# The product with w_out by groups of four token tiles, four of its seven products split once more, in matmuls of 192 columns

## The chip, the cores and the metric

One core of a Trainium2 chip. The metric is the device time of one execution in microseconds (us), and all numbers are from executions on the chip. Every run told here was in its fast state. An engine is called PE (TensorE, the matmuls), PEld (TensorE loading weights), DVE (VectorE), ACT (ScalarE), POOL (GpSimd) or SP (the queue that issues transfers).

## The reference, cut to what matters

Attention over 8 batches, 12 heads and 448 positions gives x with 3584 tokens of 768 numbers; the second half of the kernel is a feed-forward block:

```python
def _moe_ref(x, w_in, w_out):          # (3584, 768), (768, 2048), (2048, 768)
    h = x @ w_in
    g = h * (1.0 / (1.0 + np.exp(-h)))
    return (g @ w_out).astype(np.float32)
```

This case is about the last line, `g @ w_out`, in float32.

## The kernel before

A product of two matrices, each cut in 2 x 2 blocks, needs eight products of blocks. There is a form with seven products and some additions (Strassen's, in Winograd's order), and the kernel uses it for both x @ w_in and g @ w_out. `left_sums` and `right_sums` form the sums of blocks on VectorE; `Seven` runs the seven products, adds them up as they leave PSUM, and takes its PSUM banks from `bank`, which at this point of the kernel rotates over six of them:

```python
    order = ["mm", "mm", "sc", "sc", "av0", "av1"]
    def bank(n):                                    # ... (the case used earlier is cut)
        name = order[0]
        order.append(order.pop(0))
        ...
    class Seven:
        def product(self, name):
            t, ends = bank(self.n), (self.steps[0], self.steps[-1])
            for s in self.steps:
                nc.tensor.matmul(t, self.left(name, s), self.right(name, s), start=s == ends[0], stop=s == ends[1])
                yield self.n
            return t
        def five(self):
            ...
            plus((yield from self.product("6")), p1, u2)
            nc.scalar.copy(p5, (yield from self.product("5")))
            plus((yield from self.product("7")), u2, u3)
            nc.gpsimd.tensor_tensor(out=u2, in0=u2, in1=p5, op=ALU.add)
            nc.gpsimd.tensor_tensor(out=done[2, 2], in0=u3, in1=p5, op=ALU.add)
            plus((yield from self.product("3")), u2, done[1, 2])
            plus((yield from self.product("4")), u3, done[2, 1])
```

For w_out a pair of token tiles (256 tokens) is taken at a time. A block of the left side is 128 tokens by 1024 hidden numbers, so a product is eight matmuls of 128 rows and 384 columns:

```python
    def halves_out(t):
        w = tiles[t % 2].rearrange("p (m r t c) -> p m r t c", m=HF, r=2, t=2)
        ...
        left_sums(a11, a12, a21, a22, s[:, 0], s[:, 1], s[:, 2])
        ...
        steps = [2 * i + k for i in ORDER for k in range(2)]
        part = Seven(lambda name, m: lefts[name][:, m], right, steps, z.HALF, done)
        yield from chain(part.two(), part.five())
        # ... stores
    for t in range(NT // 2):                        # 14 pairs
        for _ in halves_out(t):
            pass
        fetch(t + 2)
```

Of the kernel before, what the change touches and what calls it, by code (L numbers as in the profile page):

```python
# [11 lines left out]
F32 = mybir.dt.float32  # L12
AF = mybir.ActivationFunctionType
ALU = mybir.AluOpType
# [13 lines left out]
BANK = 512  # L28
# [413 lines left out]
def store(nc, out, z, column, o, m0, *queues):  # L442


    at, queues = 0, queues or [nc.sync]
    while at < o.shape[0]:
        b, c = divmod(column + at, z.S)
        j, p = divmod(c, z.R)
        n = min(z.R - p, o.shape[0] - at)
        rows = out[ds(b * z.S, z.S), ds(m0, o.shape[1])].rearrange("(p j) m -> j p m", j=z.J)  # L450
        queues[0].dma_start(rows[j, ds(p, n)], o[ds(at, n), :])
        queues = queues[1:] + queues[:1]
        at += n
# [3 lines left out]
def bounded(  # L457
# [3 lines left out]
    P, D, R, J, S = z.P, z.D, z.R, z.J, z.S  # L461
    HW, HF = z.NW // 2, z.NF // 2
    mem = ctx.enter_context(tc.tile_pool(name="mem", bufs=1))
    ps = ctx.enter_context(tc.tile_pool(name="ps", bufs=1, space=bass.MemoryType.PSUM))
    dram = ctx.enter_context(tc.tile_pool(name="dram", bufs=1, space=bass.MemoryType.DRAM))
    NC, loads, place, norm, spare, ones, first = (
        own[name] for name in ("NC", "loads", "place", "norm", "spare", "ones", "first")
    )
# [4 lines left out]
    hidden = dram.tile([z.NF, P, z.B * S], F32, name="hidden")  # L473


    sets = [mem.tile([P, 2 * z.NW * S], F32, name=f"x{i}") for i in range(2)]
    sums_x = mem.tile([P, 3 * HW * S], F32, name="sums_x")
# [3 lines left out]
    at = 0  # L481
# [42 lines left out]
    def weights(c, j):  # L524

        return other if j == 0 and c < GROUP and c % 2 else e[j]
# [41 lines left out]
    def scores(c, j, i=None):  # L568


        banks = ps.tile([P, 2, BANK], F32, name="sc", bufs=2)
        for half in range(2):
            pair = half if j == LEFT else i
            keys = kT[:, ds((z.KA, z.KB)[0 if j == LEFT else i] + j * P, P)]
            for h in range(2):
                rows = ds(h * D, D)
                nc.tensor.matmul(  # L577
                    banks[ds(half * D, D), h, 0:S], keys[rows, ts(half, D)], qT[rows, pair, :],
                    start=True, stop=True,
                )  # L580
        for h in range(2):
            nc.scalar.activation(  # L582
                eleft[:, h] if j == LEFT else weights(c, j)[:, i, h], banks[:, h, 0:S], AF.Exp,
                scale=norm.column(c, i, h, j),
            )

# [111 lines left out]
    def minus(a, b, out):  # L698
        nc.vector.tensor_tensor(out=out, in0=a, in1=b, op=ALU.subtract)

    def plus(a, b, out):
        nc.vector.tensor_tensor(out=out, in0=a, in1=b, op=ALU.add)  # L702

    def left_sums(a11, a12, a21, a22, s1, s2, s4, steps=range(4)):

        for step in steps:
            (
                lambda: plus(a21, a22, s1),
                lambda: minus(s1, a11, s2),
                lambda: minus(a11, a21, a21),  # L710
                lambda: minus(a12, s2, s4),
            )[step]()
# [22 lines left out]
    class Seven:  # L735
# [9 lines left out]
# [3 lines that stand above are left out]
                nc.tensor.matmul(  # L748
                    t, self.left(name, s), self.right(name, s), start=s == ends[0], stop=s == ends[1]
                )  # L750
                yield self.n
            return t
# [158 lines left out]
    def chunk_out(i):  # L911

        w = home[i][0].rearrange("p (m r h k) -> p m r h k", m=2, r=2, h=2)
        s = home[i][1].rearrange("p (s m k) -> p s m k", s=3, m=2)
        return (
            w[:, :, 0, 0], w[:, :, 0, 1], w[:, :, 1, 0], w[:, :, 1, 1], s[:, 0], s[:, 1], s[:, 2]
        )

    def prepare_out(m):

        if m == HF // 2:
            fetch(0)
        for _ in range(room.CHUNK):
            rounder.open()
            yield
            rounder.round()
        if m % 2:
            right_sums(*chunk_out(ORDER[m // 2]))
        yield

    NT = z.B * S // P
    size = z.NF * 2 * P
    tiles = [work[:, ds(0, size)], sets[1][:, ds(0, size)]]
    s_tiles = [work[:, ds(size, 3 * HF * P)], sums_x[:, ds(0, 3 * HF * P)]]
    outs = [stage[:, ds(i * z.DM, z.DM)] for i in range(3)]
    outs += [room.chunk(3)[:, ts(i, z.DM)] for i in range(3)]

    def fetch(t):

        if t >= NT // 2:  # L940
            return
        dst = tiles[t % 2].rearrange("p (f c) -> p f c", f=z.NF)
        nc.sync.dma_start(
            dst, hidden[:, :, ds(t * 2 * P, 2 * P)].rearrange("f p c -> p f c")
        )

    def halves_out(t):
        w = tiles[t % 2].rearrange("p (m r t c) -> p m r t c", m=HF, r=2, t=2)
        s = s_tiles[t % 2].rearrange("p (s m c) -> p s m c", s=3, m=HF)
        a11, a12, a21, a22 = (w[:, :, i, j] for j in range(2) for i in range(2))  # L950
        left_sums(a11, a12, a21, a22, s[:, 0], s[:, 1], s[:, 2])
        lefts = {"1": a11, "2": a12, "3": s[:, 2], "4": a22, "5": s[:, 0], "6": s[:, 1], "7": a21}

        def right(name, m):
            b11, b12, b21, b22, t1, t2, t4 = chunk_out(m // 2)
            return {"1": b11, "2": b21, "3": b22, "4": t4, "5": t1, "6": t2, "7": b12}[name][
                :, m % 2
            ]

        o = [outs[(2 * t + i) % len(outs)] for i in range(2)]  # L960
        done = {(i + 1, j + 1): o[i][:, ts(j, z.HALF)] for i in range(2) for j in range(2)}
        steps = [2 * i + k for i in ORDER for k in range(2)]
        part = Seven(lambda name, m: lefts[name][:, m], right, steps, z.HALF, done)
        yield from chain(part.two(), part.five())
        for i in range(2):
            if t < NT // 2 - 1 or i == 0:
                store(nc, out, z, (2 * t + i) * P, o[i], 0)
            else:
                for j in (1, 0):
                    store(  # L970
                        nc, out, z, (2 * t + i) * P, o[i][:, ts(j, z.HALF)], j * z.HALF,
                        nc.scalar, nc.sync,
                    )


    filler = dict(work=iter(()), due=0.0, share=0.0)
# [179 lines left out]
        begun[m] = rows, part_in(group, m, rows)  # L1156
        run(begun[m][1].two())
    run(halves_in(group, range(HF), prepare_out, begun))
    fetch(1)
    for t in range(NT // 2):  # L1160
        for _ in halves_out(t):
            pass
        fetch(t + 2)


@with_exitstack
# [207 lines left out]
```

## Time and profile before

| | |
|---|---|
| median of the first three runs | 1422.76 us (1421.24 to 1424.42) |
| span of the profiled run | 1424.3 us |
| stage of w_out, first to last product | 913.5 to 1419.2 us: 505.7 us |
| PE in that stage | busy without a gap |
| DVE in that stage (913 to 1419 us) | 105.7 us busy of 506 |

The stage is read from the chain of waits: a product on PE starts where the last one ended. PE therefore sets the time, and DVE has room. The lines are in the prediction below.

### The profile page before, as it was taken

How to read it: one execution, taken by the hardware profiler on the slowest of the kernel's cores; microseconds unless marked ns; L12 is line 12 of the kernel's file. 1: busy time of each engine (PE TensorE's matmuls, PEld its weight loads, DVE VectorE, ACT ScalarE, POOL GpSimd, SP SyncE). 2: the span in 40 equal slices, each digit the busy share in tenths (PEclk: the TensorE clock that was granted, in tenths of full speed). 3: DMA queues.
4: the chain of work that ended last, by engine and by line, in shares of the span. 5: the costliest groups of instructions: out<-in, count | busy, mean ns of one | idle time of the engine just before them, and what ended most of it. 6: DMA issues, size and time to landing. Idle time of an engine off the chain costs nothing.

```text
span 1424.3 us, 16665 instructions
## 1 busy us (share of the span) xinstructions
PE 1385.2 (97%) x6273; PEld 704.1 (49%) x6273; DVE 659.7 (46%) x917; ACT 492.5 (35%) x802; POOL 365.5 (26%) x261
## 2 busy tenths in 40 slices
PE   7998999999999999999999999999999999999998
PEld 4333444444444444444444455555555555555554
DVE  3886876765645445645444776622212222222220
ACT  5875555645455445455444344200000000000000
POOL 4764442433223223223221344300000000000000
PEclk9999999999999999999999999999999999999999
DMA  7654434332223223223211465422222222222210
GB/s 179 187 152 111 120 104 144 83 94 77 76 79 95 75 84 91 77 80 93 65 53 58 152 221 177 147 91 81 81 80 82 79 77 77 73 81 74 79 53 26
DMA packets 170814, 139.22 MB, mean 98 GB/s; under 512 B 102884, under 2 KB 151396, under 8 KB 170724
## 3 DMA queue, kind: packets, MB, share of 16 engines
q1 hardware_dynamic: 170656, 138.01, 33.0%
q8 instruction: 52, 0.85, 0.3%
q14 instruction: 38, 0.31, 0.1%
q10 hardware_dynamic: 68, 0.05, 0.0%
HBM read 88.47 MB, written 41.29 MB: 91 GB/s over the span
## 4 chain that ended last, share of the span: by engine, by line
PE 88%; DVE 6%; ACT 2%; issue 2%; SPq 1%; DMA 1%; POOL 0%; DVEq 0%; ACTq 0%
PE mm L748 38%; PE sc L748 15%; PE av L748 14%; PE av L609 9%; PE sc L577 8%; DVE work L652 2%; PE sc L544 1%; PE sc L559 1%; PE sc L643 1%; PE mm L643 1%; DVE work L623 1%; ACT work L582 1%; DVE rms L396 1%; DVE W L116 1%; DVE stage L702 0%
## 5 line engine op out<-in xcount | busy, mean ns | idle before, releaser
L748 PE MATMUL mm<-x,W 128*128 128x448 f32 x654 | 264.3, 549 | 10.7 <-DVE stage L702 7.5
L582 ACT ACTIVATE work<-sc,rms 128x448 f32<-128x448 f32 x324 | 184.1, 632 | 86.4 <-PE sc L577 78.2
L424 POOL TENSOR_TENSOR rms<-rms,minus_half 128x14 f32<-128x14 f32 (+4 forms) x55 | 138.6, 2522 | 254.5 <-DVE rms L420 201.1
L748 PE MATMUL mm<-sums_x,W 128*128 128x448 f32 x474 | 190.5, 542 | 2.3 <-DVE stage L702 1.5
L748 PEld LDWEIGHTS mm<-x,W 128*128 128x128 f32 x654 | 122.2, 192 | 138.8 <-issue 109.0
L577 PE MATMUL sc<-work 64*64 64x448 f32 x1344 | 165.6, 550 | 6.9 <-ACT work L582 5.0
L609 PE MATMUL av<-work,rows 64*64 64x448 f32 x1296 | 153.8, 549 | 7.9 <-issue 2.8
L623 DVE TENSOR_TENSOR work<-work 128x896 f32<-128x896 f32 (+1 forms) x114 | 123.3, 1114 | 76.4 <-ACT work L582 75.6
L748 PEld LDWEIGHTS mm<-sums_x,W 128*128 128x128 f32 x474 | 88.6, 190 | 91.7 <-issue 83.2
L763 POOL TENSOR_TENSOR parts<-parts,stage 128x448 f32<-128x448 f32 (+1 forms) x36 | 47.7, 1324 | 328.4 <-DVE parts L702 328.4
L609 PEld LDWEIGHTS av<-work,rows 64*64 64x64 f32 x1296 | 52.2, 134 | 97.4 <-issue 87.9
L577 PEld LDWEIGHTS sc<-work 64*64 64x64 f32 x1344 | 51.9, 134 | 89.4 <-issue 38.7
L763 POOL TENSOR_TENSOR parts<-parts,W 128x384 f32<-128x384 f32 x9 | 8.9, 993 | 307.5 <-DVE parts L702 307.5
L396 DVE TENSOR_REDUCE rms<-squares 112x8 f32<-112x512 f32 (+1 forms) x80 | 52.4, 655 | 68.1 <-ACT squares L395 67.3
L748 PE MATMUL sc<-W,work 128*128 128x384 f32 x204 | 68.6, 486 | 0.0
L881 ACT ACTIVATE stage<-stage 128x896 f32<-128x896 f32 x63 | 57.2, 945 | 25.9 <-DVE stage L702 25.3
L755 ACT COPY stage<-mm 128x448 f32<-128x448 f32 (+1 forms) x29 | 15.3, 528 | 143.5 <-PE mm L748 143.5
L395 ACT ACTIVATE squares<-rows 128x512 f32<-128x512 f32 (+1 forms) x74 | 44.8, 606 | 57.8 <-DVE rms L396 56.6
L748 PE MATMUL av<-W,work 128*128 128x384 f32 x192 | 64.5, 486 | 0.0
L748 PE MATMUL mm<-W,work 128*128 128x384 f32 x192 | 64.5, 486 | 0.0
L652 DVE RECIPROCAL work<-sc 128x224 f32<-128x224 f32 x36 | 55.6, 1548 | 11.2 <-PE sc L643 11.1
L702 DVE TENSOR_TENSOR stage<-mm,parts 128x448 f32<-128x448 f32 (+1 forms) x57 | 34.6, 607 | 45.1 <-PE mm L748 29.7
(161 smaller groups left out, 1720.9 us busy)
## 6 DMA issues: line engine op xcount, KB each, us to landing
hidden<-stage SPq DMA_DIRECT2D x63, 448.0 KB, 2.8
work<-hidden SPq DMA_DIRECT2D x7, 2048.0 KB, 8.7
x<-hidden SPq DMA_DIRECT2D x7, 2048.0 KB, 8.9
rows<-in_moe_w_out_dram SPq DMA_DIRECT2D x32, 384.0 KB, 3.2
W<-in_moe_w_in_dram SPq DMA_DIRECT2D x22, 512.0 KB, 4.9
rows<-in_k_dram SPq DMA_DIRECT2D x48, 192.0 KB, 2.9
work<-work SPq DMA_DIRECT2D x144, 56.0 KB, 1.9
rows<-in_q_dram SPq DMA_DIRECT2D x36, 224.0 KB, 3.5
```

The costliest lines, as they stand in the source:

```text
L395: nc.scalar.activation(t, rows, AF.Square)
L396: nc.vector.tensor_reduce(out=out, in_=t.rearrange("p (n d) -> p n d", n=n), axis=AX.X, op=ALU.add)
L424: nc.gpsimd.tensor_tensor(out=t, in0=t, in1=half, op=ALU.pow)
L577: nc.tensor.matmul(banks[ds(half * D, D), h, 0:S], keys[rows, ts(half, D)], qT[rows, pair, :], start=True, stop=True,)
L582: nc.scalar.activation(eleft[:, h] if j == LEFT else weights(c, j)[:, i, h], banks[:, h, 0:S], AF.Exp, scale=norm.column(c, i, h, j),)
L609: nc.tensor.matmul(sums[i][ds(h * D, D), :], v, w, start=(j == 0 and step == 1), stop=(j == LEFT - 1 and step == 1),)
L623: nc.vector.tensor_tensor(out=total, in0=total, in1=more, op=ALU.add)
L652: nc.vector.reciprocal(out=r[0][:, rows], in_=t[:, rows])
L702: nc.vector.tensor_tensor(out=out, in0=a, in1=b, op=ALU.add)
L748: nc.tensor.matmul(t, self.left(name, s), self.right(name, s), start=s == ends[0], stop=s == ends[1])
L763: nc.gpsimd.tensor_tensor(out=u2, in0=u2, in1=p5, op=ALU.add)
L881: nc.scalar.activation(t, t, AF.Silu)
```

## The change

Its intent is to apply the same trick a second time. Four tiles (512 tokens) form a group, so a block of the left side is 256 tokens by 1024. Of the seven products of a group, products 4, 7, 3 and 2 are split again into seven products of their own halves, of four matmuls of 192 columns each. A split product so takes 28 matmuls of 192 columns, 5376 columns, where a whole one takes 16 of 384 (eight for each half of the group), 6144 columns: an eighth fewer. Products 1, 5 and 6 stay whole, and in the first group all seven do, while VectorE prepares the second-level sums of w_out. The core of the diff:

```diff
+    banks = ctx.enter_context(ExitStack())
+    ps = banks.enter_context(tc.tile_pool(name="ps", bufs=1, space=bass.MemoryType.PSUM))
 ...
+    DEEP = (4, 7, 3, 2)
 ...
+    def deep(name, out, then=lambda t, h: None):
+        a = deep_left(name)
+        def product(of):
+            t = ps_out.tile([P, BANK], F32, name="seventh", bufs=6)[:, 0:QUARTER]
+            for i in ORDER:
+                x, y = of_seven(of, a, deep_right(name, i))
+                nc.tensor.matmul(t, x[:, i], y, start=i == ORDER[0], stop=i == ORDER[-1])
+            return t
+        nc.scalar.copy(p1, product(1))
+        plus(product(2), p1, out[:, 0, 0])
+        ...                                          # 6, 5, 7, two additions on GpSimd, 4, 3
 ...
+    def single(name, t):
+        o = ps_out.tile([P, BANK], F32, name="one", bufs=2)[:, 0 : z.HALF]
+        ...                                          # eight matmuls of 384 columns
 ...
+    def quad(q):                                     # one group; cut to its order
+        which = DEEP if q > 0 else ()
+        def spread(t=None):
+            add_pool(c12, c22, c12)                  # three additions of 768 columns on GpSimd
+            add_pool(c22, x, c22)
+            add_pool(c21, x, c21)
+            ...                                      # stores
+        p1 = [single(1, 0), single(1, 1)]
+        ...                                          # single 5, deep(4), single 6
+        if 7 in which:
+            left_sums(*deep_left(3))
+            deep(7, aside[0])
+            plus(aside[0], c[1, 2], aside[0])
+            spread()
+        ...
+        if 2 in which:
+            left_sums(*deep_left(2))
+        if 3 in which:
+            deep(3, aside[1])
+        ...                                          # deep(2), stores
-    for t in range(NT // 2):
-        for _ in halves_out(t):
-            pass
-        fetch(t + 2)
+    banks.close()
+    ps_out = ctx.enter_context(tc.tile_pool(name="ps_out", bufs=1, space=bass.MemoryType.PSUM))
+    for q in range(QUADS):                           # 7 groups
+        quad(q)
```

More of the change, by code (lines that the diff above doesn't have):

```diff
@@ L463, in bounded @@
     mem = ctx.enter_context(tc.tile_pool(name="mem", bufs=1))
-    ps = ctx.enter_context(tc.tile_pool(name="ps", bufs=1, space=bass.MemoryType.PSUM))
     dram = ctx.enter_context(tc.tile_pool(name="dram", bufs=1, space=bass.MemoryType.DRAM))
+    banks = ctx.enter_context(ExitStack())
+    ps = banks.enter_context(tc.tile_pool(name="ps", bufs=1, space=bass.MemoryType.PSUM))
     NC, loads, place, norm, spare, ones, first = (
@@ L568, in scores @@
     def scores(c, j, i=None):
-        banks = ps.tile([P, 2, BANK], F32, name="sc", bufs=2)
+        two = ps.tile([P, 2, BANK], F32, name="sc", bufs=2)
         for half in range(2):
@@ L577, in scores @@
                 nc.tensor.matmul(
-                    banks[ds(half * D, D), h, 0:S], keys[rows, ts(half, D)], qT[rows, pair, :],
+                    two[ds(half * D, D), h, 0:S], keys[rows, ts(half, D)], qT[rows, pair, :],
                     start=True, stop=True,
@@ L582, in scores @@
             nc.scalar.activation(
-                eleft[:, h] if j == LEFT else weights(c, j)[:, i, h], banks[:, h, 0:S], AF.Exp,
+                eleft[:, h] if j == LEFT else weights(c, j)[:, i, h], two[:, h, 0:S], AF.Exp,
                 scale=norm.column(c, i, h, j),
@@ L921, in prepare_out @@
         if m == HF // 2:
-            fetch(0)
+            for at in ((0, 0), (1, 0), (1, 1)):
+                fetch(0, *at)
         for _ in range(room.CHUNK):
@@ L931, in bounded @@
     NT = z.B * S // P
-    size = z.NF * 2 * P
-    tiles = [work[:, ds(0, size)], sets[1][:, ds(0, size)]]
-    s_tiles = [work[:, ds(size, 3 * HF * P)], sums_x[:, ds(0, 3 * HF * P)]]
-    outs = [stage[:, ds(i * z.DM, z.DM)] for i in range(3)]
-    outs += [room.chunk(3)[:, ts(i, z.DM)] for i in range(3)]
-    def fetch(t):
-        if t >= NT // 2:
-            return
-        dst = tiles[t % 2].rearrange("p (f c) -> p f c", f=z.NF)
-        nc.sync.dma_start(
-            dst, hidden[:, :, ds(t * 2 * P, 2 * P)].rearrange("f p c -> p f c")
-        )
@@ L947, in halves_out @@
-    def halves_out(t):
-        w = tiles[t % 2].rearrange("p (m r t c) -> p m r t c", m=HF, r=2, t=2)
-        s = s_tiles[t % 2].rearrange("p (s m c) -> p s m c", s=3, m=HF)
-        a11, a12, a21, a22 = (w[:, :, i, j] for j in range(2) for i in range(2))
-        left_sums(a11, a12, a21, a22, s[:, 0], s[:, 1], s[:, 2])
-        lefts = {"1": a11, "2": a12, "3": s[:, 2], "4": a22, "5": s[:, 0], "6": s[:, 1], "7": a21}
-        def right(name, m):
-            b11, b12, b21, b22, t1, t2, t4 = chunk_out(m // 2)
-            return {"1": b11, "2": b21, "3": b22, "4": t4, "5": t1, "6": t2, "7": b12}[name][
-                :, m % 2
-            ]
-        o = [outs[(2 * t + i) % len(outs)] for i in range(2)]
-        done = {(i + 1, j + 1): o[i][:, ts(j, z.HALF)] for i in range(2) for j in range(2)}
-        steps = [2 * i + k for i in ORDER for k in range(2)]
-        part = Seven(lambda name, m: lefts[name][:, m], right, steps, z.HALF, done)
-        yield from chain(part.two(), part.five())
-        for i in range(2):
-            if t < NT // 2 - 1 or i == 0:
-                store(nc, out, z, (2 * t + i) * P, o[i], 0)
-            else:
-                for j in (1, 0):
-                    store(
-                        nc, out, z, (2 * t + i) * P, o[i][:, ts(j, z.HALF)], j * z.HALF,
-                        nc.scalar, nc.sync,
-                    )
@@ new lines, in bounded, with take @@
+    QUADS = NT // 4
+    QUARTER = z.HALF // 2
+    assert NT % 4 == 0
+    regions = [
+        work, sets[1], sums_x, room.chunk(3), room.sums(3), stage, ring, parts
+    ]
+    regions = [[a, 0] for a in regions]
+    def take(n, *which):
+        for i in which:
+            a, at = regions[i]
+            if at + n <= a.shape[1]:
+                regions[i][1] += n
+                return a[:, ds(at, n)]
+        raise AssertionError
+    size = HF * 2 * P
+    left = {(0, 0): take(size, 0), (1, 0): take(size, 0), (1, 1): take(size, 0)}
@@ new lines, in bounded @@
+    left[0, 1] = take(size, 1)
+    left_sum = take(size, 2)
+    deep_lefts = [take(3 * size // 4, 3) for _ in range(2)]
+    DEEP = (4, 7, 3, 2)
+    deep_rights = {
+        name: take(3 * 4 * QUARTER, *at).rearrange("p (s i k) -> p s i k", s=3, i=4)
+        for name, at in zip(DEEP, ([4], [6], [1], [5]))
+    }
+    results = {at: take(2 * z.HALF, i) for at, i in (((1, 1), 0), ((2, 2), 0), ((2, 1), 6), ((1, 2), 6))}
+    aside = [take(2 * z.HALF, 2) for _ in range(2)]
+    copies = [[take(QUARTER, 1, 7) for _ in range(4)] for _ in range(2)]
@@ new lines, in fetch, with sums_left @@
+    def fetch(q, i, r):
+        if q >= QUADS:
+            return
+        dst = left[i, r].rearrange("p (f c) -> p f c", f=HF)
+        source = hidden.rearrange("(f r) p c -> r p f c", r=2)
+        nc.sync.dma_start(dst, source[r, :, :, ds((4 * q + 2 * i) * P, 2 * P)])
+    LEFTS = {
+        1: left[0, 0], 2: left[0, 1], 3: left_sum, 4: left[1, 1],
+        5: left_sum, 6: left_sum, 7: left[1, 0],
+    }
+    def sums_left(*which):
+        a11, a12, a21, a22, x = (
+            a.rearrange("p (n c) -> p n c", n=2)
+            for a in (left[0, 0], left[0, 1], left[1, 0], left[1, 1], left_sum)
+        )
+        for n in range(2):
+            left_sums(
+                *(a[:, n] for a in (a11, a12, a21, a22)), x[:, n], x[:, n], x[:, n], which
+            )
@@ new lines, in right_one, with deep_left, deep_right @@
+    def right_one(name, i):
+        b11, b12, b21, b22, t1, t2, t4 = chunk_out(i)
+        return {1: b11, 2: b21, 3: b22, 4: t4, 5: t1, 6: t2, 7: b12}[name]
+    def deep_left(name):
+        a = LEFTS[name].rearrange("p (i m t c) -> p m t i c", i=4, m=2, t=2)
+        s = deep_lefts[DEEP.index(name) % 2].rearrange("p (s i c) -> p s i c", s=3, i=4)
+        return a[:, 0, 0], a[:, 1, 0], a[:, 0, 1], a[:, 1, 1], s[:, 0], s[:, 1], s[:, 2]
+    def deep_right(name, i):
+        b = right_one(name, i)
+        s = deep_rights[name]
+        h = [ts(k, QUARTER) for k in range(2)]
+        return b[:, 0, h[0]], b[:, 0, h[1]], b[:, 1, h[0]], b[:, 1, h[1]], s[:, 0, i], s[:, 1, i], s[:, 2, i]
@@ new lines, in sums_deep_right, with of_seven @@
+    def sums_deep_right(name, last):
+        for i in ORDER:
+            b11, b12, b21, b22, t1, t2, t4 = deep_right(name, i)
+            if last:
+                minus(b22, b12, b12)
+            else:
+                minus(b12, b11, t1)
+                minus(b22, t1, t2)
+                minus(b21, t2, t4)
+    def of_seven(name, a, b):
+        a11, a12, a21, a22, s1, s2, s4 = a
+        b11, b12, b21, b22, t1, t2, t4 = b
+        return {
+            1: (a11, b11), 2: (a12, b21), 3: (s4, b22), 4: (a22, t4),
+            5: (s1, t1), 6: (s2, t2), 7: (a21, b12),
+        }[name]
@@ new lines, in deep @@
+    def deep(name, out, then=lambda t, h: None):
+        a = deep_left(name)
+        out = out.rearrange("p (t h k) -> p t h k", t=2, h=2)
+        p1, u2, u3, p5 = copies[DEEP.index(name) % 2]
+        def product(of):
+            t = ps_out.tile([P, BANK], F32, name="seventh", bufs=6)[:, 0:QUARTER]
+            for i in ORDER:
+                x, y = of_seven(of, a, deep_right(name, i))
[3 more added lines that the diff above has]
+        plus(product(2), p1, out[:, 0, 0])
+        then(0, 0)
+        plus(product(6), p1, u2)
+        nc.scalar.copy(p5, product(5))
+        plus(product(7), u2, u3)
+        add_pool(u2, p5, u2)
+        add_pool(u3, p5, out[:, 1, 1])
+        plus(product(4), u3, out[:, 1, 0])
+        then(1, 1)
+        then(1, 0)
+        plus(product(3), u2, out[:, 0, 1])
+        then(0, 1)
@@ new lines, in single, with save_out @@
+    def single(name, t):
+        a = LEFTS[name].rearrange("p (f t c) -> p f t c", f=HF, t=2)
+        o = ps_out.tile([P, BANK], F32, name="one", bufs=2)[:, 0 : z.HALF]
+        steps = [(i, m) for i in ORDER for m in range(2)]
+        for n, (i, m) in enumerate(steps):
+            nc.tensor.matmul(
+                o, a[:, 2 * i + m, t], right_one(name, i)[:, m],
+                start=n == 0, stop=n == len(steps) - 1,
+            )
+        return o
+    def save_out(q, i, j, t):
+        store(
+            nc, out, z, (4 * q + 2 * (i - 1) + t) * P, results[i, j][:, ts(t, z.HALF)],
+            (j - 1) * z.HALF,
+        )
@@ new lines, in both, with add_pool, last @@
+    def both(f):
+        for t in range(2):
+            f(t)
+    def add_pool(a, b, o):
+        nc.gpsimd.tensor_tensor(out=o, in0=a, in1=b, op=ALU.add)
+    def quad(q):
+        c = results
+        half = lambda a, t: a[:, ts(t, z.HALF)]
+        which = DEEP if q > 0 else ()
+        def spread(t=None):
+            x, c12, c22, c21 = (
+                a if t is None else half(a, t) for a in (aside[0], c[1, 2], c[2, 2], c[2, 1])
+            )
+            add_pool(c12, c22, c12)
+            add_pool(c22, x, c22)
+            add_pool(c21, x, c21)
+            for k in range(2) if t is None else (t,):
+                save_out(q, 2, 2, k)
+                save_out(q, 2, 1, k)
+        p1 = [single(1, 0), single(1, 1)]
+        fetch(q, 0, 1)
+        sums_left(0, 2)
+        both(lambda t: nc.scalar.copy(half(c[1, 1], t), p1[t]))
+        if q == 0:
+            sums_deep_right(4, False)
+        both(lambda t: nc.scalar.copy(half(c[2, 2], t), single(5, t)))
+        if 4 in which:
+            left_sums(*deep_left(4))
+        sums_left(1)
+        fetch(q + 1, 0, 0)
+        if 4 in which:
+            left_sums(*deep_left(7))
+            deep(4, c[2, 1])
+        else:
+            both(lambda t: nc.scalar.copy(half(c[2, 1], t), single(4, t)))
+            sums_deep_right(7, False)
+            sums_deep_right(4, True)
+        fetch(q + 1, 1, 1)
+        for t in range(2):
+            plus(single(6, t), half(c[1, 1], t), half(c[1, 2], t))
+        sums_left(3)
+        if 7 in which:
[3 more added lines that the diff above has]
+            spread()
+        else:
+            for t in range(2):
+                plus(single(7, t), half(c[1, 2], t), half(aside[0], t))
+                spread(t)
+            sums_deep_right(3, False)
+            sums_deep_right(7, True)
+        fetch(q + 1, 1, 0)
+        if 2 in which:
+            left_sums(*deep_left(2))
+        if 3 in which:
+            deep(3, aside[1])
+            add_pool(c[1, 2], aside[1], c[1, 2])
+            both(lambda t: save_out(q, 1, 2, t))
+        else:
+            for t in range(2):
+                plus(single(3, t), half(c[1, 2], t), half(c[1, 2], t))
+                save_out(q, 1, 2, t)
+            sums_deep_right(2, False)
+            sums_deep_right(3, True)
+        if q == QUADS - 1:
+            def last(t, h):
+                columns = ds((2 * t + h) * QUARTER, QUARTER)
+                rows = c[1, 1][:, columns]
+                plus(rows, aside[0][:, columns], rows)
+                store(
+                    nc, out, z, (4 * q + t) * P, rows, h * QUARTER,
+                    *((nc.scalar, nc.sync)[:: 1 if h else -1]),
+                )
+            deep(2, aside[0], last)
+        elif 2 in which:
+            deep(2, aside[0])
+            add_pool(c[1, 1], aside[0], c[1, 1])
+            both(lambda t: save_out(q, 1, 1, t))
+        else:
+            for t in range(2):
+                plus(single(2, t), half(c[1, 1], t), half(c[1, 1], t))
+                save_out(q, 1, 1, t)
+        if q == 0:
+            sums_deep_right(2, True)
@@ L1158, in bounded @@
     run(halves_in(group, range(HF), prepare_out, begun))
-    fetch(1)
-    for t in range(NT // 2):
-        for _ in halves_out(t):
-            pass
-        fetch(t + 2)
+    banks.close()
+    ps_out = ctx.enter_context(tc.tile_pool(name="ps_out", bufs=1, space=bass.MemoryType.PSUM))
+    for q in range(QUADS):
+        quad(q)
 @with_exitstack
```

## The prediction

> **What bounds the kernel now.** I read the page first: the span, the busy tenths by slice, and the chain that ended last.
>
> ```profile
> span 1424.3 us, 16665 instructions
> PE   7998999999999999999999999999999999999998
> DVE  3886876765645445645444776622212222222220
> ACT  5875555645455445455444344200000000000000
> PEclk9999999999999999999999999999999999999999
> PE 88%; DVE 6%; ACT 2%; issue 2%; SPq 1%; DMA 1%; POOL 0%; DVEq 0%; ACTq 0%
> ```
>
> TensorE is full in nearly every slice and carries 88% of the chain. In the last third, from about 914 us, which is the product with w_out that the change rewrites, VectorE is at two tenths and ScalarE near nothing. A time saved on TensorE there is saved on the whole, as long as no other engine is drawn in. The chain in order of time shows how tight that stage is (start, length, work):
>
> ```profile
> 913.49 10.32 PE sc L748 x32
> 923.81 10.32 PE av L748 x32
> 934.13 10.32 PE mm L748 x32
> ...
> 1388.21 10.32 PE av L748 x32
> 1398.53 10.32 PE mm L748 x32
> 1408.85 10.33 PE sc L748 x32
> ```
>
> Each piece begins where the last one ended: no wait at all from 913.5 to 1419.2. One float32 matmul leaves two records, so a product of eight matmuls is 16 records, and 32 records in 10.32 us make 0.3225 us a record and 5.16 us a product. There are 14 pairs of token tiles with seven products each: 98 x 5.16 = 505.7 us, which is the stage.
>
> Next I read the timeline where this stage begins, because the change closes the PSUM pool there and opens another.
>
> ```profile
> 913.33 1.45 PE L748 MATMUL sc<-x,work 128*128 128x384 f32 x4
> ```
>
> ```profile
> 910.99 2.69 DVE L699 TENSOR_TENSOR W<-W 128x768 f32<-128x768 f32 x3 [0.88 <-POOL W L124]
> 913.60 0.61 DVE L702 TENSOR_TENSOR parts<-av,parts 128x448 f32<-128x448 f32 x1
> 915.52 0.62 DVE L702 TENSOR_TENSOR stage<-mm,parts 128x448 f32<-128x448 f32 x1 [1.30 <-POOL parts L763]
> 916.61 0.62 DVE L702 TENSOR_TENSOR stage<-mm,parts 128x448 f32<-128x448 f32 x1 [0.47 <-POOL stage L764]
> 917.16 1.22 DVE L702 TENSOR_TENSOR work<-work 128x1024 f32<-128x1024 f32 x1
> ```
>
> TensorE starts on w_out at 913.33, but VectorE reads the last three w_in products out of PSUM only between 913.60 and 917.23: it was held up by sums of w_out and by two GpSimd additions. Before the change nobody cares, since six banks rotate. Last, I looked at what a gap of TensorE does to its clock, in stretches early in the kernel (columns: stretch, its length, busy PE, PEld, DVE, ACT, POOL, granted clock, DMA share, GB/s):
>
> ```profile
> 107.30:109.90 2.60, 0.00 (x0) 0.00 (x0) 2.53 (x6) 0.00 (x0) 0.41 (x1) 0.87 0.75 171
> 109.30:116.00 6.70, 6.05 (x20) 2.22 (x24) 3.76 (x4) 0.87 (x2) 1.28 (x1) 0.50 0.29 97
> 242.40:245.70 3.30, 3.30 (x6) 1.66 (x5) 2.58 (x4) 0.00 (x0) 0.00 (x0) 0.50 0.44 145
> 246.00:250.00 4.00, 4.00 (x27) 1.71 (x29) 0.69 (x1) 3.09 (x5) 0.00 (x0) 1.00 0.53 194
> ```
>
> Two gaps of 2.7 us (107.2 to 109.95 and 239.2 to 241.9) were each followed by half clock, for about 6.8 us and 3.4 us.
>
> [...] The trace has 1219 ns at 1024 columns and 557 at 384[...]; so I take 0.69 us for 512 columns, 0.36 for 192, 0.96 for 768.
>
> **The change, part by part.** Token tiles go in seven groups of four. The first group is ordinary: 7 products x 2 tiles x 5.16 = 72.2 us, as two pairs cost now; it also makes the second-level sums of w_out. In the other six, products 1, 5 and 6 stay whole: 6 x 5.16 = 30.96 us. Products 4, 7, 3 and 2 become seven products each, of four matmuls with 192 columns: 28 matmuls x 2 records x 0.1625 = 9.10 us instead of 10.32; four of them 36.40 us. A group is 67.36 us instead of 72.24, 4.88 less, and six groups save 29.3 us. These matmuls are more in number (1072 for 784) and fewer in columns (x 13/14 in six groups).
>
> Does the rest keep up? VectorE in a group of 67.4 us: left sums 8 x 1.22 = 9.8, second-level left sums 16 x 0.69 = 11.1, evictions 20 x 0.36 + 2 x 0.56 = 8.3, one sum of 768 columns 0.96: 30 us, under half. GpSimd: its additions took 0.99 us at 384 columns and 1.13 at 448, so by a straight line (estimate) 1.83 at 768 and 0.57 at 192: 5 x 1.83 + 8 x 0.57 = 13.7 us. I then laid the order of instructions against these durations. The tightest place is product 7: after product 6 VectorE has 2.4 us of left sums and 2.8 us of second-level sums to do before it evicts, while the six small banks last 6 x 1.3 = 7.8 us; it holds. The left sum of product 5 must be ready 10.3 us into the group, and VectorE needs 3.7 us for it once the transfer of the third quarter has landed. That transfer is issued some 8 us before the group ends, behind eight stores at about 0.4 us of issue each; a transfer of twice the size lands in 8.8 us, so this holds with several us to spare. In the first group the second-level sums of w_out are 64 x 0.36 = 23 us, spread over 72. So within the groups I expect TensorE to stay dense.
>
> At the seam it will not. In the built program the first matmul of the new stage waits for the last VectorE eviction of the old one, since all old banks must be free before the new pool's first one is. That eviction ended at 917.23. With some 0.2 us for the signal and the weight load, TensorE restarts near 917.45 instead of 913.33: 4.1 us lost. A gap longer than the two of 2.7 us will draw half clock. Of a half-clock time of 3.4 to 6.8 us, less what falls in the gap, half is lost: 1.7 to 3.1 us; I take 2.3.
>
> The end: now one eviction of 384 columns (0.56 us), then a store. After: eviction 0.36, a sum of 192 columns 0.36, then a smaller store: +0.1.
>
> Sum: 1422.8 - 29.3 + 4.1 + 2.3 + 0.1 = 1400.0 us, which is 1.6% less.
>
> **The rivals.** First, the weight load becomes the bound. A 190 ns weight-load record is longer than 162.5 ns; if records could not overlap, six groups x 224 records x 27.5 ns = 37 us would be added, about 1437 us. Against it are the warm-up matmuls[...] (kind, duration ns min/median/max; then the run of them):
>
> ```profile
> L342 PEld LDWEIGHTS idle<-ident x24: 286/333/333, 1.4 to 7.9; 128*128 128x128 f32 x24
> ```
>
> ```profile
> 4.78 3.48 PEld L342 LDWEIGHTS idle<-ident 128*128 128x128 f32 x16
> ```
>
> Each record is 333 ns long, yet 16 take 3.48 us, so they start (3.48 - 0.33) / 15 = 0.21 us apart: a full load hides behind a matmul of 128 columns, and here it has 192. I give this 5%. Second, the seam costs nothing (a bank is free early, or the last evictions come sooner): 1393.6 us, just over 2% faster. The order of waits in the program speaks against it. Third, a wait inside the groups, most likely of VectorE for a transfer or of a product for a late eviction: with 2 us a group, 1412 us. The slacks above speak against it, but I laid them by hand. Fourth, the seam costs its gap without any half clock: 1397.7 us.
>
> **Range and chances.** The saving of 29.3 us is sure to about 1 us, the seam is between 4 and 9 us, and unplanned waits add 0 to 6. That gives 1400 us, and 1395.5 to 1405 eight times in ten. The 2% line is at 1394.3, under the range: it needs a seam of under 1 us. Faster by over 2%: 0.10; within 2%: 0.86; slower by over 2%: 0.04.
>
> **What would show it.** In the changed trace: records of 192 columns 0.1625 us apart, so 56 in 9.10 us; groups two to seven about 67.4 us apart; at the seam one TensorE gap of about 4 us whose releaser is the last VectorE eviction, then a stretch at clock 0.50; VectorE at four to five tenths in the last third. Records about 0.19 us apart would mean the weight load binds; TensorE gaps inside the groups would mean a wait that I missed; no gap at the seam would put the result over the 2% line.

Of its figures, 1219 and 557 ns are VectorE's float32 tensor_tensor at 1024 and 384 columns in the trace of before (L699, L702), and 0.69, 0.36 and 0.96 us are estimates: a straight line through those two gives 0.69, 0.36 and 0.95. The 162.5 ns for a record of 192 columns is one too: in that trace records of 448 columns start 0.376 us apart and of 384 columns 0.3225, and a straight line through these gives 0.162. The 0.2 us for the signal and the weight load is an estimate; the load's record alone is 0.19 us. The warm-up, at 0.21 us a load, shows that weight loads overlap, but not that they can follow each other 0.1625 us apart: this was first shown by the trace of the changed kernel.

## The result, and the profile after

Median 1399.24 us (1397.43 to 1402.15, four runs), beside 1422.99 us of the kernel before. The ratio is 0.9836, with a 95% interval of 0.9813 to 0.9858; a ratio here is the mean time of one kernel's fast runs over that of the other's of the same rounds, so it is not quite the ratio of the two medians. The kernel is faster by 1.6%, clear of the noise and under the 2% line. The result is correct. Five further rounds gave a median of 1402.86 us and a ratio of 0.9856 (below).

The page of the changed kernel, the same lines as the prediction shows of before, and weight loads as well:

```profile
span 1395.6 us, 18420 instructions
PE   7998999999999999999999999989999999999998
PEld 4333444444444444444444455555687879696967
DVE  3887876765644444644444686654554545454635
```

PE is still full, except for one 8 among the nines: that is where the stage begins. DVE went from two tenths to about five, PEld from five to between six and nine. The chain of waits, over the seam and one group and a half (start, length, work):

```profile
910.63 0.64 DVE stage L703
911.27 0.04 issue
911.32 93.15 PE one L1060 x288
1004.46 9.10 PE seventh L1037 x56
1013.56 10.32 PE one L1060 x32
1023.88 18.20 PE seventh L1037 x112
1042.08 0.01 issue
1042.09 9.37 PE seventh L1037 x56
1051.46 20.64 PE one L1060 x64
```

Three things are to be seen. A split product is 56 records (28 float32 matmuls, two records each) in 9.10 us, 0.1625 us each, where a whole one took 10.32. The chain now leaves PE for DVE just before the stage. And the last split product of a group, product 2, takes 9.37 us: 0.27 us too long. The timeline of PE at the seam gives the first gap its length and its releaser (in brackets):

```profile
905.09 2.42 PE L749 MATMUL mm<-sums_x,W 128*128 128x448 f32 x6
911.32 1.56 PE L1060 MATMUL one<-x,work 128*128 128x384 f32 x4 [3.81 <-DVE stage L703]
```

The granted clock (the figure after the busy times) in the gap and after it, for this run:

```profile
907.60:911.20 3.60, 0.00 (x0) 0.00 (x0) 1.83 (x5) 0.95 (x1) 2.21 (x2) 1.00 0.00 0
911.40:920.00 8.60, 8.60 (x27) 5.15 (x28) 8.26 (x16) 1.32 (x2) 0.00 (x0) 1.00 0.67 229
```

There is no half clock here (experiment 1 sets it beside a trace that has it). Last, the timeline of DVE and POOL between products 7 and 2 of the second group, and the weight load that starts product 2:

```profile
1034.43 0.68 DVE L703 TENSOR_TENSOR W<-x 128x512 f32<-128x512 f32 x1
1034.59 2.19 POOL L1077 TENSOR_TENSOR rows<-rows,work 128x768 f32<-128x768 f32 x1 [2.53 <-DVE sums_x L703]
1035.15 2.19 DVE L700 TENSOR_TENSOR W<-W,x 128x512 f32<-128x512 f32 x1
1036.86 2.14 POOL L1077 TENSOR_TENSOR work<-work,sums_x 128x768 f32<-128x768 f32 x1
1037.25 2.30 DVE L700 TENSOR_TENSOR x<-x 128x512 f32<-128x512 f32 x1
1038.96 2.26 POOL L1077 TENSOR_TENSOR rows<-rows,sums_x 128x768 f32<-128x768 f32 x1
1039.47 2.30 DVE L700 TENSOR_TENSOR W<-x,W 128x512 f32<-128x512 f32 x1
1041.69 0.34 DVE L703 TENSOR_TENSOR sums_x<-seventh,x 128x192 f32<-128x192 f32 x1
...
1042.09 0.30 PEld L1037 LDWEIGHTS seventh<-x,x 128*128 128x128 f32 x2 [0.31 <-DVE sums_x L703]
```

The first DVE sum of 512 columns, which began before the addition on POOL, takes 0.68 us. The other three, which began while an addition ran on POOL, take 2.2 to 2.3 us, and each of them ends about 0.55 us after the POOL addition beside it: as if the work began only when POOL had finished. The eviction at 1041.69 is late by this, and the weight load that starts product 2 waits 0.31 us for it. The total of this wait over the stage was 1.8 us, six times.

Where the 28.7 us between the two profiled spans came from, by the two chains (PE's last w_in product ended at 913.49 before and at 903.00 + 4.51 = 907.51 after):

| part | before, us | after, us | difference |
|---|---|---|---|
| to the end of the last w_in product | 913.5 | 907.5 | -6.0 |
| seam and w_out, to the end of the last product | 505.7 | 482.15 | -23.5 |
| from there to the end | 5.1 | 5.9 | +0.8 |

The first row is not the change's doing. The run of before had half clock after its two early gaps (the prediction shows it), the run of after had not: from 107.3 to 116.0 us and from 236 to 246 us its granted clock was 1.00. Runs of one kernel differ in this (the first four of the change have mean granted clocks of 0.994 to 0.998), and this makes the pair of profiles differ by more than the medians do.

### The profile page after: what moved, and what is told of

Same layout as the page of the kernel before. It is cut to its first block, busy times and chain, and to the rows that moved or that the text cites. A ratio compares the mean times of both kernels' runs of the same rounds, so it can differ in the third digit from the quotient of the medians.

```text
span 1395.6 us, 18420 instructions
## 1 busy us (share of the span) xinstructions
PE 1352.6 (97%) x6849; PEld 775.0 (56%) x6849; DVE 799.7 (57%) x1157; ACT 509.0 (36%) x852; POOL 433.7 (31%) x316
## 4 chain that ended last, share of the span: by engine, by line
PE 87%; DVE 6%; ACT 2%; issue 2%; DMA 1%; SPq 1%; POOL 0%; DVEq 0%; ACTq 0%; POOLq 0%
PE mm L749 26%; PE one L1060 19%; PE seventh L1037 16%; PE av L610 9%; PE sc L578 8%; PE av L749 3%; PE sc L749 3%; DVE work L653 2%; PE sc L545 1%; PE sc L560 1%; PE mm L644 1%; PE sc L644 1%; DVE rms L396 1%; DVE work L624 1%; ACT work L583 1%
## 5 line engine op out<-in xcount | busy, mean ns | idle before, releaser
L749 PE MATMUL mm<-x,W 128*128 128x448 f32 x654 | 261.0, 543 | 10.6 <-DVE stage L703 7.4
L1060 PE MATMUL one<-W,sums_x 128*128 128x384 f32 x360 | 121.0, 486 | 0.0
L1060 PEld LDWEIGHTS one<-W,sums_x 128*128 128x128 f32 x360 | 68.4, 190 | 47.7
L764 POOL TENSOR_TENSOR parts<-parts,stage 128x448 f32<-128x448 f32 x31 | 42.4, 1368 | 168.3 <-DVE parts L703 168.2
L1060 PE MATMUL one<-W,work 128*128 128x384 f32 x216 | 72.6, 486 | 0.0
L1040 ACT COPY x<-seventh 128x192 f32<-128x192 f32 x24 | 7.6, 318 | 156.6 <-PE seventh L1037 151.2
L1077 POOL TENSOR_TENSOR x<-x 128x192 f32<-128x192 f32 x12 | 7.1, 591 | 177.0 <-DVE x L703 177.0
L700 DVE TENSOR_TENSOR sums_x<-sums_x,work 128x1024 f32<-128x1024 f32 x14 | 17.2, 1226 | 72.1 <-PE one L1060 71.7
```

The costliest lines, as they stand in the source:

```text
L1060: nc.tensor.matmul(o, a[:, 2 * i + m, t], right_one(name, i)[:, m], start=n == 0, stop=n == len(steps) - 1,)
```

## The experiments

The disputed points were the seam (whether its gap draws half clock, and whether the gap can be had away), the 0.3 us stall (whether POOL causes it), the whole gain (whether the columns alone bring it) and the time of a still shorter matmul. Each run was made in the same rounds as the kernel before, on the same chip; the rounds were on three chips (experiments 1 to 4; 5, the first form of 6, and 7; the repeats and the mended form of 6), so runs of different rounds are compared by their ratios.

**1. The changed kernel again** (no edit).

> The changed kernel itself, again, for a closer time and a second trace of the seam. Theory A[...]: runs scatter between about 1397 and 1403 us with the mean granted clock between 0.998 and 0.994, and this trace may or may not show clock 0.50 just after the seam; the first one did not. Theory B (no half clock ever comes at this seam): the stretch after the seam is at clock 1.00 in this trace too, and the scatter comes from the first 250 us. Both: median 1398 to 1401 us, gap at the seam 3.8 us, groups 67.64 us apart.

Median 1402.86 us (1400.61 to 1404.15), ratio 0.9856 (0.9841 to 0.9871). The gap at the seam was 3.8 us as before, but here it was followed by half clock:

```profile
913.65:917.07 3.42, 0.70 (x2) 0.49 (x3) 2.00 (x3) 1.67 (x2) 2.01 (x2) 1.00 0.01 5
917.07:920.48 3.41, 3.41 (x7) 1.81 (x6) 3.34 (x4) 0.23 (x1) 0.00 (x0) 0.50 0.99 328
920.48:923.89 3.41, 3.41 (x12) 2.03 (x11) 3.22 (x9) 0.31 (x1) 0.00 (x0) 1.00 0.71 243
```

The same 288 records took 94.84 us here, against 93.15 in the first trace: 1.7 us lost, which is half of 3.4. Theory B is out: the same gap was followed by half clock here and not in the first trace. Of the six traces of kernels with this gap of 3.8 us (the first, this one, and the runs named sums, whole twice and 96 columns below) five point to a stretch of 3.4 us at half clock after it. In two the granted clock shows it: in this run, and in sums, where it is 0.89 over 905 to 920 us and the 288 records took 94.84 us too. In the other three it is an estimate: in whole twice the first piece is 1.96 us longer than its records at 0.3225 us, against 0.27 in the first trace, and in 96 columns the 72 records of one<-x,work, the first of the stage among them, have a mean of 510 ns, against 487 in the first trace. The median was above the 1398 to 1401 us that were expected, and two runs were above 1403: the granted clock of the four runs was 0.993 to 0.996, against 0.994 to 0.998 in the first four. The mean granted clock of this run's trace is 0.994 over 1402.4 us, that of the first trace 0.998 over 1395.6 us: 8.4 us of full clock withheld against 2.8 (an estimate, from rounded means), beside 6.8 us between the two spans.

What PE did just before a fall of the clock was read from the traces of before and of after. In their records of the granted clock, which begin at 10.2 and 11.7 us, all changes lie whole multiples of 3.413 us apart: in before at 17.07, 23.90, 109.23, 116.06, 242.35, 245.77 and 1423.36 us from the start of the span, in after at 18.49, 21.91 and 1394.06 us. Cut into stretches of this length from these times, before shows three falls while there was work (columns as in the prediction):

```profile
13.66:17.07 3.41, 1.39 (x16) 0.21 (x8) 0.00 (x0) 0.94 (x2) 0.00 (x0) 1.00 0.93 233
17.07:20.49 3.42, 1.53 (x8) 0.31 (x8) 1.72 (x4) 3.24 (x6) 1.49 (x1) 0.50 1.04 330
105.82:109.23 3.41, 1.40 (x10) 0.30 (x2) 2.83 (x4) 0.99 (x2) 0.00 (x0) 1.00 0.93 260
109.23:112.65 3.42, 2.70 (x4) 1.17 (x4) 3.42 (x4) 0.00 (x0) 1.28 (x1) 0.50 0.37 142
238.94:242.35 3.41, 0.73 (x2) 0.30 (x2) 3.41 (x4) 0.00 (x0) 1.55 (x2) 1.00 0.54 192
242.35:245.77 3.42, 3.42 (x6) 1.69 (x5) 2.63 (x4) 0.00 (x0) 0.00 (x0) 0.50 0.43 144
```

and after shows one, and a stretch that was followed by none:

```profile
15.08:18.49 3.41, 0.98 (x8) 0.21 (x8) 0.86 (x2) 2.06 (x5) 0.00 (x0) 1.00 1.10 341
18.49:21.91 3.42, 3.16 (x16) 0.86 (x20) 0.86 (x2) 3.07 (x7) 3.20 (x3) 0.50 1.15 313
233.53:236.95 3.42, 1.45 (x4) 0.38 (x2) 3.42 (x4) 0.00 (x0) 2.65 (x2) 1.00 0.79 217
236.95:240.36 3.41, 2.77 (x8) 1.47 (x9) 3.41 (x6) 0.21 (x1) 0.00 (x0) 1.00 0.73 221
```

PE was busy for 41, 41 and 21% of the stretch before a fall in before and for 29% in after; both kernels end with one more fall, after a stretch with no work. From there on no stretch of these two traces that was at clock 1.00 with PE busy for 42% or more was followed by a fall. In this run the stretch just before the fall held 0.70 us of PE work (the first line above), 20%. In the first trace the gap at the seam lay nearly evenly over two such stretches:

```profile
905.96:909.37 3.41, 1.55 (x5) 0.45 (x3) 2.29 (x4) 0.00 (x0) 0.98 (x1) 1.00 0.00 0
909.37:912.79 3.42, 1.48 (x5) 0.95 (x6) 2.75 (x4) 1.90 (x2) 1.23 (x2) 1.00 0.24 94
```

These are busy for 45 and 43%, and the clock stayed. Every stretch that drew none held at least 1.45 us of work, so the gap took less than about 2.0 us from it; a gap of 3.8 us does so only if it is cut about as evenly as here (an estimate from these two traces).

**2. No wait at the seam.** The first group keeps the rotation over the old banks, and the new pool opens after it.

```diff
-        o = ps_out.tile([P, BANK], F32, name="one", bufs=2)[:, 0 : z.HALF]
+        if alone:
+            o = bank(z.HALF)
+        else:
+            o = ps_out.tile([P, BANK], F32, name="one", bufs=2)[:, 0 : z.HALF]
 ...
+    quad(0)
+    alone = False
     banks.close()
     ps_out = ...
-    for q in range(QUADS):
+    for q in range(1, QUADS):
         quad(q)
```

> The first group of four tiles still takes its PSUM banks from the old pool in rotation; the new pool opens after it, where the last product is evicted at once. Theory: the wait for the late VectorE evictions leaves TensorE's path; the gap of 3.8 us at the seam is gone and a gap of about 1 us appears 72 us later, so 3 us less than the changed kernel, plus what half clock the old gap drew at times (0 to 3 us): about 1395 us. Rival (VectorE's late evictions were only where an unavoidable wait showed, and it comes back as a wait inside the first group): about 1399 us.

Median 1395.96 us (1394.69 to 1397.95), ratio 0.9815, in the same rounds as experiment 1. Run once more later, with the expectation

> The seam experiment again, beside the one with both changes on the same chip. Theory: 1395 to 1397 us; from the start of the last stage to the end of its last product 479.0 us, as in its first run.

it gave 1396.91 us (1395.76 to 1397.25), ratio 0.9805. In the chain of its first trace PE goes from w_in to w_out without a break, and the new pool costs one eviction:

```profile
970.91 10.33 PE sc L1063 x32
981.25 0.02 issue
981.27 0.57 DVE work L703
981.84 0.04 issue
981.88 20.91 PE one L1063 x64
```

So the wait for the late evictions was real and could be had away; it did not come back inside the first group. Against experiment 1 in the same rounds the ratios differ by 0.0041, 5.8 us on 1422.6: at the upper end of the 3 to 6 us that were expected (the gap, and at times half clock).

**3. The sums ahead of GpSimd's additions.** The same operations in another order.

```diff
             deep(7, aside[0])
+            left_sums(*deep_left(2))
             plus(aside[0], c[1, 2], aside[0])
             spread()
 ...
-        if 2 in which:
-            left_sums(*deep_left(2))
         if 3 in which:
```

> VectorE's second-level left sums for product 2 are put ahead of the three GpSimd additions of 768 columns instead of beside them; the arithmetic is the same. Theory[...]: three of these sums fall from about 2.2 us each to 0.69, the late evictions of product 3 come in time, and the TensorE gap of 0.3 us before product 2 goes in six groups: 1.7 us less, about 1397.5 us, groups 67.36 us apart. Rival (these sums are slow for their own access pattern or because of transfers): they stay at 2.2 us and the time at 1399.

The chain of its trace, one group:

```profile
1008.96 9.10 PE seventh L1037 x56
1018.06 10.32 PE one L1060 x32
1028.38 27.30 PE seventh L1037 x168
```

Products 7, 3 and 2 are 168 records in 27.30 us, which is 3 x 9.10: the stall is gone. The timeline of DVE and POOL shows why:

```profile
1038.58 0.69 DVE L700 TENSOR_TENSOR W<-W,x 128x512 f32<-128x512 f32 x1
1039.19 0.69 DVE L700 TENSOR_TENSOR x<-x 128x512 f32<-128x512 f32 x1
1039.79 0.69 DVE L700 TENSOR_TENSOR W<-x,W 128x512 f32<-128x512 f32 x1
```

The same three sums take 0.69 us each, and the POOL additions, which now run beside evictions from PSUM, 1.81 us instead of 2.1 to 2.3. The same holds over the whole stage of the first trace: all 18 subtractions of 512 columns (L700) that overlap a POOL instruction took 2.18 to 2.30 us, all 54 that overlap none 0.68 to 0.69. Transfers were absent there: the DMA share was 0.00 from 1035.15 to 1039.00 us, over the first slow sum and most of the second. So neither the access pattern nor a transfer made them slow; POOL did. The five sums of 1024 columns (L700) that overlap a POOL instruction took 2.71 us, the 36 that overlap none 1.22. Evictions from PSUM did not change: 36 of 192 columns overlap a POOL instruction and took 0.36 us, 84 overlap none and took 0.34 to 0.36. The median was 1399.58 us (1398.23 to 1400.71), ratio 0.9837 against 0.9856 of experiment 1 in the same rounds: 2.7 us less where 1.7 was expected, with intervals that overlap. The time alone would not have decided, since 1399 is what the rival had said; the trace does.

**4. A longer gap at the seam.** Eight more DVE operations ahead of the last evictions.

```diff
+        if m == HF - 1:
+            for _ in range(8):
+                nc.vector.tensor_tensor(out=spare, in0=spare, in1=spare, op=ALU.max)
         yield
```

> Eight extra VectorE operations of 512 columns (0.69 us each, 5.5 us together) are put ahead of the last evictions of the old stage, to lengthen the gap at the seam from 3.8 to about 9.3 us[...]. Theory A[...]: clock 0.50 for 3.4 us or more after the seam in the trace, and the time goes up by 5.5 us of gap plus about 1.7 us of half clock or more: about 1406 to 1407 us. Theory B (no half clock comes at this place): only the gap, about 1404.5 us, and clock 1.00 after it.

Median 1410.8 us (1407.06 to 1411.14), 7.9 us above experiment 1. The gap was 9.5 us, and half clock lay over its end and past it:

```profile
917.30:927.40 10.10, 4.93 (x8) 2.81 (x9) 8.20 (x11) 1.90 (x2) 2.21 (x2) 0.50 0.42 144
927.50:937.00 9.50, 9.50 (x31) 5.56 (x30) 3.67 (x11) 0.96 (x2) 0.00 (x0) 1.00 0.14 49
```

PE started again at 922.47, so about 5 us of work ran at half clock, a loss of about 2.5 us beside the 5.7 us by which the gap grew. The spans of the two traces differ by 6.9 us; the gap and the half clock (2.5 less the 1.7 of experiment 1) account for 6.5. Theory A, half clock after the longer gap, holds. The median is above the 1406 to 1407 that was written, since that was reckoned from the first median of 1399.

**5. Experiments 2 and 3 together.** Both edits, nothing else.

> The old PSUM pool kept for the first group, as in the seam experiment, together with the second-level left sums of product 2 ahead of the GpSimd additions. If the two act in different places their gains add: 1396.0 of the seam experiment less 1.7, about 1394.3 us, groups 67.36 us apart, no half clock in the last third. Rival (the 0.3 us stall only moves elsewhere when the first group starts earlier): 1396.

Median 1395.96 us (1394.41 to 1396.50), ratio 0.9809. From the start of the stage to the end of the last product it took 477.3 us (911.13 to 1388.46) against 479.0 in experiment 2 (908.99 to 1387.99), so the two gains add in the stage, but the whole was not clearly shorter. Therefore both were run side by side:

> Both changes again. Theory: the last stage takes 477.3 us against 479.0 of the seam experiment, and the whole is 1.7 us shorter than that one on the average of the same rounds, if the half clock of the first 250 us, which differs from run to run by some us, evens out. Rival: no difference in the whole.

The stage took 477.3 us again (910.79 to 1388.11), against 479.0 (910.38 to 1389.37) of the seam experiment. The whole took 1395.33 us (1393.71 to 1396.36), ratio 0.9793 (0.9779 to 0.9807), beside 1396.91 us and 0.9805 (0.9791 to 0.9819) of the seam experiment: 0.0012 on 1423.5 is 1.7 us, as in the stage, though the intervals of the two overlap. It is the fastest version tried, and correct: at the 2% line (its interval holds 0.98), 0.4 to 0.6% under the two medians of the change as it stands, by the ratios.

**6. The products left whole.** The structure of groups, banks, transfers and stores, with no split product.

```diff
-        which = DEEP if q > 0 else ()
+        which = ()
 ...
     def sums_deep_right(name, last):
-        for i in ORDER:
+        for i in ():
```

> The four products of each group are left whole again (and the second-level sums of w_out left out); groups of four tiles, the seam and the stores stay as in the change. Theory (all of the gain is the fewer columns on TensorE): groups of 72.24 us, so the kernel before plus the seam: 4.0 us of gap and 0 to 2 us of half clock, about 1427 to 1429 us. Rival (part of the gain is from the new order of transfers and stores): clearly under 1426.

Median 1427.28 us, ratio 1.0028, but the result was wrong (relative error 0.28): the last product of the last group has its own branch and was still split, without its sums. The mended form adds

```diff
-        if q == QUADS - 1:
+        if q == QUADS - 1 and which:
```

> The mended form of the run with all products whole, which had left the last product of the last group split (without its sums, hence wrong) and so was 1.2 us too short. Theory: 72.24 us in all seven groups, the seam as in the change: the kernel before plus 4.0 us and 0 to 2 us of half clock, 1427 to 1429 us, and a correct result. Rival as before: under 1426.

Correct, with a median of 1429.52 us (1427.95 to 1430.06), ratio 1.0035 (1.0018 to 1.0052). The chain after the seam is a single piece:

```profile
914.51 507.65 PE one L1060 x1568
```

1568 records at 0.3225 us are 505.7 us, and the other 2 us are put down to the restart (0.27 us in the first trace) and one stretch of half clock (1.7 us in experiment 1). Without the split products the change loses 5.0 us by the ratio and 6.0 by the medians, where 4 to 6 were expected. All of its gain is thus the fewer columns on PE.

**7. Matmuls of 96 columns.** Each small matmul is issued as two halves with the same weights, which are loaded anew for each.

```diff
-                nc.tensor.matmul(t, x[:, i], y, start=i == ORDER[0], stop=i == ORDER[-1])
+                for part in range(2):
+                    columns = ts(part, QUARTER // 2)
+                    nc.tensor.matmul(
+                        t[:, columns], x[:, i], y[:, columns],
+                        start=i == ORDER[0] and part == 0, stop=i == ORDER[-1] and part == 1,
+                    )
```

> Each matmul of 192 columns is issued as two of 96 with the same weights, so that each loads its weights again; 112 records in a split product instead of 56. If only the columns count, records are 0.0825 us apart[...] and a split product takes 9.24 us: about 1403 us.[...] If the whole 190 ns record were the floor, 21.3 us and about 1690 us; that was the rival of the prediction, and it would then have been seen at 192 columns too.

Two runs, 1481.34 and 1482.15 us, correct. In the chain:

```profile
1008.31 12.48 PE seventh L1039 x112
1020.79 10.35 PE one L1065 x32
```

112 records in 12.48 us are 0.111 us a record. That is neither the 0.0825 us of the columns (an estimate; a straight line through 0.3225 us at 384 columns and 0.1625 at 192 gives the same) nor the 0.192 us of a weight-load record here: with a load of 128 float32 columns for every record, this stream went at 111 ns a record. The run does not tell the load itself from another cost of each record. A fixed cost of 111 ns for any record is ruled out, since in the trace of before transposes with a load each (L544) start 96 ns apart. At 192 columns records are 162.5 ns apart, some 50 ns more than loads of this kind needed here.

## Why the prediction was right

It said 1400.0 us, and 1399.24 was measured, by mostly the terms that it had summed. That the two are only 0.8 us apart is luck: the same kernel, run again, was at 1402.86.

- *Split products at 9.10 us, six groups save 29.3 us.* Right: 56 records in 9.10 us, the starts of the groups 67.64 us apart, of which 0.28 is the stall. Experiment 6 shows the other side: without them nothing is gained.
- *The weight load stays hidden.* Right: with a load each, records of 192 columns were 162.5 ns apart. Experiment 7 refutes the rival at 1437 us as well: there loads of 128 columns followed each other 111 ns apart.
- *The seam loses 4.1 us of PE.* Right to the tenth: 911.32 - 907.51 = 3.8 us, and 0.27 us in the first piece (93.15 us for 288 records at 0.3225) make 4.1. Experiment 2 shows that the cause named, the late evictions, is the cause.
- *Half clock after it, 2.3 us.* That it can follow is right, the size and the certainty are off. It came in five of six traces by experiment 1, as a single stretch of 3.4 us each time: 1.7 us where it came, none in the trace of the first run, so 1.4 us on the average of these six. The prediction had reckoned with every gap over 2.7 us drawing it; this gap of 3.8 us drew none in one trace. In the first trace its fourth rival, a gap without half clock, is what happened.
- *TensorE dense within the groups.* Nearly: the term that was left out is 0.28 us a group, 1.7 us in all; this is the late eviction of the third rival, which had put 2 us a group on it. The step that failed is the account of VectorE, 0.69 us for each second-level sum: three in four of those for product 2 took 2.2 to 2.3 us beside GpSimd, and the line of slacks laid by hand missed the place, product 2, where this told. VectorE and GpSimd were counted one by one, and never against each other: in the group from 1051.5 to 1119.1 us DVE was busy 34.4 us where 30 was written, and the three slow sums, 1.5 to 1.6 us too long each, make up the difference. A sum of 1024 columns was slow too, 2.71 us beside GpSimd where 1.22 was written; no product waited for it. (The slow sums come to more than the difference, as busy time counts overlapping records once.)
- *The end, +0.1.* It was +0.8: from the end of the last product to the end of the kernel 5.9 us against 5.1. DVE's part is as predicted; the rest is after the last store was issued, and no experiment looked into it. In experiment 6 mended, where the last product is whole, it was 5.7 us (1422.17 to 1427.9), but there the last two stores were issued one after the other on one queue, in 1.20 us, so that run does not tell whether the small last stores are the reason. This stays open.

The two small misses, +1.7 for the stall and +0.7 for the end, stand against 0.9 less of half clock, and together lie within the scatter of the runs, which is 3 to 5 us wide in the kernel before as well. The range of 1395.5 to 1405 held: the eight runs of the change lie between 1397.43 and 1404.15.

## What to carry to other kernels

When a change cuts work on the engine that sets the end, the work is paid for on others: count not only how busy each is, but which of them run at the same moment, and order apart those that slow each other. Here VectorE's sums of 512 columns took 2.2 to 2.3 us beside GpSimd's additions and 0.69 alone; another order cost nothing and removed a stall. A change of pools between two stages waited here for the last eviction of the first, 3.8 us; look up when its last reader finishes, not when its last writer does, and put the change where the last reader is prompt. Shorter matmuls paid here at 192 columns, with 162.5 ns a record, and no longer at 96, with 111 ns where the columns alone would give 82.5 (an estimate): try the size before you count on its columns. The same gap of 3.8 us was followed by half clock in five traces of six by experiment 1, so one trace of a gap does not tell what the gap costs.
